# Chunk 0 of a delta-rule kernel: 64-token inverses from 16-token blocks by four 64-row products per head instead of seven of 32 rows

## The chip, the core and the metric

The program runs on one core of one Trainium2 chip. The metric is device time in microseconds of one execution. The engines are named as in the profile: PE is the matrix engine, PEld its weight loads, DVE the vector engine, ACT the scalar engine, POOL GpSimd, SP the engine that issues most transfers.

## What is computed

Four batches of eight heads of 768 tokens and head size 48 go through a delta rule, and its result through a feed-forward layer with 384 inputs and 2048 hidden units.

```python
k_n = k / (norm(k) + 1e-06)
for t in range(S):
    y[:, :, t] = einsum('bhd,bhde->bhe', q[:, :, t], state)
    v_old = einsum('bhde,bhd->bhe', state, k_n[:, :, t])
    state = state + beta_t * einsum('bhd,bhe->bhde', k_n[:, :, t], v_t - v_old)
x = y.transpose(0, 2, 1, 3).reshape(B * S, H * D)
h = x @ w_in
out = (h * sigmoid(h)) @ w_out
```

## The kernel before

**Chunks and halves.** The 768 tokens are worked in six chunks of 128, each chunk in two halves of 64 (`W`). Within a half the recurrence is written as a triangular system for each of the 32 pairs of batch and head (`BH`): the scores of the keys with each other above the diagonal, times a step size for each token, give a unit triangular matrix of 64x64, whose inverse (scaled by the step sizes) is kept in `xi`, 64 rows for each head, `[128, 2 groups, 16 heads, 64]`. With it, `inner` turns values into updates, `update` adds these to the state, and `keys`, `old`, `new` and `first_outputs` read state and scores. The two halves of a chunk and the two groups of batches lie crosswise on the upper and lower 64 partitions (`on`, `heads`).

**Inverses of chunk 0.** The score blocks go out to memory (`block_out`, by `issue`) and come back with one head's 32x32 block a partition (`block_in`, L570). `invert_first` (L651) scales them by the step sizes (L656), runs 15 rank-one steps on the two 16x16 corners of every block at once (L664, L668), scales again (L671), and transposes the result twice on DVE (L678 and L682) to have tokens on partitions again. Then three stages, made by generators, join 16 to 32 tokens on PE: `corner` (L705), `turned` (L721) and `straight` (L734), and `merge_half` (L794) twice joins 32 to 64. Every stage writes products of 32 rows into two PSUM banks, which ACT and DVE copy out (`by_act` L532, `by_dve` L535, and L712). For each half that is seven products a head and 32 heads; a product of 32-bit data is two records of the trace. `joins(0)` runs as a whole before the first half of chunk 0 is solved. `joins(1)`, for the second half, is drawn piecewise by the script.

**Step sizes.** `norm_steps(0)` (L391 to L421, DVE) makes the key norms, `spread` and the sizes by slot. `block_steps` (L430) brings `spread` to one head's block a partition by a product (`pg`, L433) and a copy on ACT (`step`, L438). `first_queries(b)` transposes queries of batch `b` on PE (L488), copies on ACT (L498), multiplies scores (L517) and masks them on DVE (L527, b below 2) or copies on ACT.

**Order of work.** Each engine does its instructions in program order: every instruction is pinned behind the last one on its engine (`pin`), and transfers on SP stand in one line (`in_line`), some of them behind the landing of the one before (`linked`). `busy` puts filler products on PE (L336); in the loop of the inverse's steps they wait for a DVE step. The weights `w_in` and `w_out` are fetched in eight pieces each and narrowed piece by piece (`fill`; ACT L224 and L225, DVE L229 and L233, POOL L237); a `hidden` product (L1029) of step r needs piece r // 2. POOL also squares keys (L373), clears `xi` (L1303), the identity blocks (L552) and `slab` (L1337), copies `pick` (L679) and scales values (`size_half`, L445).

**The script.** After `joins(0)` a text gives the order of everything else around chunks 0 and 1, word by word: `s` a step of `solve` (first `inner` L828 of the first half, then `first_outputs` L872 twice, `update` L848, `keys` L816, `old` L894, `new` L907), `jN` N steps of `joins(1)`, `r` a step of the feed-forward of chunk 0 (three `hidden` products), `f` a step of narrowing, `b` the begin of a piece, `q` the queries of chunk 1, `W` and `w` fetches, `h` the scaling of the second half's values. L1326 masks the query scores of batches 2 and 3, ahead of the script.

Of the kernel before, what the change touches and what calls it, by code (L numbers as in the profile page):

```python
# [19 lines left out]
def kernel(  # L20
# [19 lines left out]
    W = 64  # L40
# [223 lines left out]
    AT_G = 0  # L264
    AT_X = AT_G + (T + 1) * T
    AT_UP = AT_X + SLAB
    AT_LOW = AT_UP + BH * T
    AT_LAST = 2 * HFF * HM
    assert AT_LOW + BH * T // 2 <= 3 * HFF * HM and BH * T <= HFF * HM
# [56 lines left out]
    second = const.tile([P, 1], FP32, name="second")  # L326
    pin(nc.vector.tensor_reduce(out=second[:], in_=pick[:, T // 2 : T], axis=AX.X, op=ALU.add))
    xi = const.tile([P, 2, HH, W], FP32, name="xi")
    xis = [xi[:, g] for g in range(2)]
    crossed = const.tile([P, HH, T], FP32, name="crossed")  # L330

# [209 lines left out]

    def block_room(c):

        if c == 0:
            g, x = (sum_room[:, at : at + T * T] for at in (AT_G, AT_X))
        else:
            g = work.tile([P, T * T], FP32, name="g", tag="g", bufs=1)[:]
            x = (
                sum_room[:, AT_LAST : AT_LAST + T * T] if c == 1
                else work.tile([P, T * T], FP32, name="x", tag="x", bufs=1)[:]  # L550
            )
# [3 lines left out]
        blocks[c] = (tc.dram_tile([P, T, T], FP32, name=f"blocks{c}"), g, x)  # L555
# [89 lines left out]
    Q, ys = T // 2, {}  # L645
# [4 lines left out]

    def invert_first(step):  # L651

        x = blocks.pop(0)[2]
        g2, x2 = corners(AT_G), corners(AT_X)
# [4 lines left out]
        for m in range(Q - 1, 0, -1):  # L659
# [14 lines left out]
        rows = [slice(T * j, T * (j + 1)) for j in range(NB)]  # L674
        low = sum_room[:, AT_LOW : AT_LOW + BH * Q].rearrange("p (n s) -> p n s", s=Q)
        y = sum_room[:, AT_G : AT_G + BH * T].rearrange("p (n s) -> p n s", s=T)
        up = sum_room[:, AT_UP : AT_UP + BH * T].rearrange("p (n t) -> p n t", t=T)
# [7 lines left out]
        both = work.tile([P, BH, T], FP32, name="xe_y", tag="g", bufs=1)  # L685
        xes[0], ys[0] = both[:], both[:].rearrange("p (g h) t -> p g h t", g=2)

        def heads(g, hf):
            for i in range(HH // 2):
                for e in range(2):  # L690
                    yield i, HH * g + 2 * i + e, hf ^ e ^ g

        def of_half(t, g, hf, k):
            return t[:, HH * g + (hf ^ k ^ g) : HH * (g + 1) : 2]

        def out_of(pl, to, width):
            return pl[to, 0 : HH // 2 * width].rearrange("p (n s) -> p n s", s=width)

        def corner(g, hf):

            pls = [bank(room, "pl") for room in (A, CC)]
            for i, n, k in heads(g, hf):
                for j in (2 * k, 2 * k + 1):
                    cols = slice(T * (j % 2), T * (j % 2 + 1))
                    pin(nc.tensor.matmul(  # L705
                        pls[k][rows[j], Q * i : Q * (i + 1)], lhsT=aps[0, g][0][rows[j], n % HH // H, n % H, cols],
                        rhs=low[rows[j], n, :], start=True, stop=True,
                    ))
                    yield
            for k in range(2):  # L710
                of = slice(W * k, W * (k + 1))
                pin(nc.vector.scalar_tensor_tensor(  # L712
                    out=of_half(y[of], g, hf, k)[:, :, 0:Q], in0=out_of(pls[k], of, Q), scalar=second[of],
                    in1=pick[of, 0:Q].unsqueeze(1).to_broadcast([W, HH // 2, Q]), op0=ALU.mult, op1=ALU.add,
                ))

        def turned(g, hf):

            pls = [bank(room, "pl") for room in (A, CC)]
            for i, n, k in heads(g, hf):  # L720
                pin(nc.tensor.matmul(  # L721
                    pls[k][rows[2 * k], T * i : T * (i + 1)], lhsT=up[rows[2 * k], n, :],
                    rhs=y[rows[2 * k], n, :], start=True, stop=True,
                ))
                yield
            for k, by in enumerate((by_act, by_dve)):
                by(of_half(xes[0][rows[2 * k]], g, hf, k), out_of(pls[k], rows[2 * k], T))

        def straight(g, hf):

            pls = [bank(room, "pl") for room in (A, CC)]
            for i, n, k in heads(g, hf):
                for j in (2 * k + 1, 2 * k):
                    pin(nc.tensor.matmul(  # L734
                        pls[k][rows[j], T * i : T * (i + 1)], lhsT=y[rows[j], n, :],
                        rhs=up[rows[j], n, :], start=True, stop=True,
                    ))
                    yield
            for odd in (1, 0):
                for k, by in enumerate((by_act, by_dve)):  # L740
                    j = 2 * k + odd
                    by(
                        of_half(xi[rows[j]].rearrange("p g h t -> p (g h) t"), g, hf, k)[:, :, T * odd : T * odd + T],
                        out_of(pls[k], rows[j], T),
                    )

        yield corner, turned, straight
# [3 lines left out]
    slab = sum_room[:, AT_X : AT_X + SLAB]  # L751
# [28 lines left out]

    def merge_half(g, hf, second):

        y = ys[0][:, g]
        pms = [bank(room, "px" if second else "py") for room in (A, CC)]
        for i in range(HH // 2):
            for e in range(2):
                n, k = 2 * i + e, hf ^ e ^ g
                even, odd = slice(W * k, W * k + T), slice(W * k + T, W * (k + 1))
                if second:
                    to, left, right = even, y[odd, n, :], xis[g][odd, n, T:W]  # L790
                else:
                    left = aps[0, g][0][even, n // H, n % H, T:W]
                    to, right = odd, xes[0][even, g * HH + n, :]
                yield pin(nc.tensor.matmul(  # L794
                    pms[k][to, T * i : T * (i + 1)], lhsT=left, rhs=right, start=True, stop=True
                ))
        for k, by in enumerate((by_act, by_dve)):
            e, half = hf ^ k ^ g, slice(W * k, W * k + T) if second else slice(W * k + T, W * (k + 1))
            of = pms[k][half, 0 : HH // 2 * T].rearrange("p (h t) -> p h t", t=T)
            by(xis[g][half, e::2, T:W] if second else y[half, e::2, :], of)  # L800
# [486 lines left out]
    def first_queries(b):  # L1287

        def evacuate(j, e, to, of):
            (mask if b < HB else by_act)(to, of)  # L1290

        turn(0, b, 1, M)
        score(0, b, (1,), (A, CC), evacuate)
# [42 lines left out]
    corner, turned, straight = next(inv)  # L1336
    pin(nc.gpsimd.memset(slab, 0.0))  # L1337

    def joins(hf, between=()):

        for stage in (
            corner(0, hf), corner(1, hf), turned(0, hf), turned(1, hf), straight(0, hf), merge_half(0, hf, False),
            straight(1, hf), merge_half(1, hf, False), merge_half(0, hf, True), merge_half(1, hf, True),
        ):
            yield from stage
            for what in between[:1]:
                what()
            between = between[1:]
# [4 lines left out]
    def sized():  # L1353
        size_half(0, pins[seen_on])
        begin_next()
# [88 lines left out]
    def script(text):  # L1444

        nonlocal pieces
        for word in text.split():
# [12 lines left out]
            elif what == "j":  # L1460
                go(rest, n)
            elif what == "q":
# [96 lines left out]
```

## Time and profile before

| What | us |
|---|---|
| three runs | 652.4, 662.53, 659.86 |
| their median | 659.86 |
| the profiled execution | 652.37 |
| its span, first to last instruction | 650.4 |
| PE busy | 627.6 (96%) |
| DVE busy | 397.6 (61%) |
| ACT busy | 213.8 (33%) |
| POOL busy | 90.9 (14%) |
| first rank-one scaling of chunk 0 (L656) starts | 20.71 |
| first join product (L705) starts | 33.37 |
| `inner` of the first half (L828) starts | 44.24 |
| first `hidden` product (L1029) starts | 52.34 |
| xT of the second half lands | 101.17 |

Times are from the span's start. A row of a timeline has start, length, engine, line, operation, `out<-in`, shape and count, and in brackets the idle time before it with what ended it; "issue" means that nothing in the profile shows what was waited for. The granted clock is the share of full speed that PE was allowed. Counts of matmuls are of records, and a few of them are missing in the trace.

### The profile page before, as it was taken

How to read it: one execution, taken by the hardware profiler on the slowest of the kernel's cores; microseconds unless marked ns; L12 is line 12 of the kernel's file. 1: busy time of each engine (PE TensorE's matmuls, PEld its weight loads, DVE VectorE, ACT ScalarE, POOL GpSimd, SP SyncE). 2: the span in 40 equal slices, each digit the busy share in tenths (PEclk: the TensorE clock that was granted, in tenths of full speed). 3: DMA queues.
4: the chain of work that ended last, by engine and by line, in shares of the span. 5: the costliest groups of instructions: out<-in, count | busy, mean ns of one | idle time of the engine just before them, and what ended most of it. 6: DMA issues, size and time to landing. Idle time of an engine off the chain costs nothing.

```text
span 650.4 us, 21395 instructions
## 1 busy us (share of the span) xinstructions
PE 627.6 (96%) x9416; PEld 548.0 (84%) x9416; DVE 397.6 (61%) x911; ACT 213.8 (33%) x497; POOL 90.9 (14%) x92
## 2 busy tenths in 40 slices
PE   7878899999989999999999999999999999999997
PEld 5577778756779989989989989989989989889997
DVE  5875689997764987453986453987454974103112
ACT  2455663332342122451122452122451122451111
POOL 5023631334101020010020010020011000000000
PEclk9979999999989999999999999999999999999999
DMA  9876534250288324268324268324173024100101
GB/s 136 209 165 206 192 75 104 98 97 3 53 154 148 58 73 60 50 136 143 59 76 57 48 131 146 61 74 60 28 153 72 10 65 60 40 13 1 25 0 25
DMA packets 145676, 54.70 MB, mean 84 GB/s; under 512 B 117152, under 2 KB 138912, under 8 KB 145584
## 3 DMA queue, kind: packets, MB, share of 16 engines
q1 hardware_dynamic: 143136, 52.93, 39.6%
q8 instruction: 74, 1.21, 0.8%
q10 hardware_dynamic: 2448, 0.41, 0.4%
q14 instruction: 18, 0.15, 0.1%
HBM read 40.14 MB, written 11.01 MB: 79 GB/s over the span
## 4 chain that ended last, share of the span: by engine, by line
PE 91%; DMA 2%; issue 2%; DVE 2%; ACT 1%; SPq 1%; DVEq 0%
PE phid L1029 38%; PE px L1136 16%; PE py L1136 12%; PE po L1064 5%; PE pb_c L828 3%; PE pa L517 2%; PE pb_c L816 2%; PE pyc L907 2%; PE pb_c L1064 2%; PE pb_c L848 1%; PE pb_c L336 1%; PE pyc L894 1%; DMA kb<-in_k_dram 1%; PE pt L488 1%; PE py L770 1%
## 5 line engine op out<-in xcount | busy, mean ns | idle before, releaser
L1029 PE MATMUL phid<-xT,w_in 128*128 128x256 f32 x1152 | 260.1, 383 | 2.1 <-DMA xT<-part 2.0
L1029 PEld LDWEIGHTS phid<-xT,w_in 128*128 128x128 f32 x1152 | 216.9, 191 | 34.4 <-issue 3.0
L1039 ACT ACTIVATE gT<-phid 128x512 f32<-128x512 f32 x88 | 52.5, 597 | 149.8 <-PE phid L1029 145.2
L615 DVE SCALAR_TENSOR_TENSOR rank<-g,step,x 128x31 f32<-128x31 f32 (+15 forms) x124 | 49.8, 401 | 35.8 <-DMA g<-blocks 32.3
L1118 DVE TENSOR_TENSOR sums_of_g<-gT 128x384 f32<-128x384 f32 (+1 forms) x60 | 29.9, 518 | 59.0 <-ACT gT L1039 48.4
L1136 PE MATMUL py<-w_out,sums_of_g 128*128 128x192 f32 x320 | 56.8, 329 | 0.0
L1136 PE MATMUL px<-sums_of_w,sums_of_g 128*128 128x192 f32 x320 | 56.8, 329 | 0.0
L1136 PEld LDWEIGHTS px<-sums_of_w,sums_of_g 128*128 128x128 f32 x320 | 52.2, 190 | 0.5
L1136 PEld LDWEIGHTS py<-w_out,sums_of_g 128*128 128x128 f32 x320 | 52.2, 190 | 0.4
L620 DVE TENSOR_TENSOR x<-x,rank 128x31 f32<-128x31 f32 (+15 forms) x124 | 42.5, 343 | 4.3
L455 POOL TENSOR_TENSOR vf<-vf,n_slot 128x768 f32<-128x768 f32 x10 | 15.0, 1516 | 169.3 <-DMA vf<-in_v_dram 125.3
L476 DVE STREAM_TRANSPOSE kq<-stage 128x512 f32<-128x512 f32 x28 | 28.5, 1114 | 12.0 <-DMA stage<-in_q_dram 10.4
L532 ACT COPY xT<-pyc 48x128 f32<-48x128 f32 (+2 forms) x126 | 32.6, 259 | 1.6
L1136 PE MATMUL px<-sums_of_w,gT 128*128 128x192 f32 x160 | 28.4, 329 | 0.0
L1136 PE MATMUL py<-w_out,gT 128*128 128x192 f32 x160 | 28.4, 329 | 0.0
L1136 PE MATMUL px<-w_out,gT 128*128 128x192 f32 x160 | 28.0, 327 | 0.0
L1136 PEld LDWEIGHTS px<-w_out,gT 128*128 128x128 f32 x160 | 26.4, 190 | 0.5
L538 POOL COPY g<-x 64x256 f32<-64x256 f32 x4 | 5.0, 1241 | 154.5 <-DVE x L623 154.5
L1136 PEld LDWEIGHTS py<-w_out,gT 128*128 128x128 f32 x160 | 26.1, 190 | 0.3
L1136 PEld LDWEIGHTS px<-sums_of_w,gT 128*128 128x128 f32 x160 | 26.1, 190 | 0.2
L828 PEld LDWEIGHTS pb_c<-vf,xi 64*64 64x64 f32 x736 | 23.5, 138 | 3.2 <-issue 2.9
L1147 DVE TENSOR_TENSOR o<-o,kept 128x192 f32<-128x192 f32 (+1 forms) x29 | 11.5, 422 | 24.0 <-ACT kept L1144 24.0
(221 smaller groups left out, 921.6 us busy)
## 6 DMA issues: line engine op xcount, KB each, us to landing
vf<-in_v_dram SPq DMA_DIRECT2D x48, 96.0 KB, 3.2
out_dram<-o SPq DMA_DIRECT2D x42, 96.0 KB, 2.2
w_out<-in_moe_w_in_dram SPq DMA_DIRECT2D x4, 768.0 KB, 4.4
sums_of_w<-in_moe_w_out_dram SPq DMA_DIRECT2D x4, 768.0 KB, 5.9
blocks<-ap SPq DMA_DIRECT2D x44, 64.0 KB, 1.9
g<-blocks SPq DMA_DIRECT2D x5, 512.0 KB, 3.5
kb<-in_k_dram SPq DMA_DIRECT2D x12, 192.0 KB, 5.1
kb<-in_k_dram SPq DMA_DIRECT2D x24, 96.0 KB, 4.6
```

The source lines that it names most:

```text
L455: pin(nc.gpsimd.tensor_tensor(out=vf, in0=vf, in1=of, op=ALU.mult))
L476: pin(nc.vector.transpose(out=kqs[c, b][:, :, j, :].rearrange("p a (i m) -> p a m i", i=T), in_=src.rearrange("p a (m d) -> p a m d", d=D) ...
L517: pin(nc.tensor.matmul(pa[e][half, p * n * W : (p + 1) * n * W], lhsT=kq[rows, p, 0, half], rhs=kq[rows, p, js[0] : js[-1] + 1, half], sta ...
L532: return pin(nc.scalar.copy(to, of))
L615: pin(nc.vector.scalar_tensor_tensor(out=tv, in0=g[:, 0:m, m : m + 1].to_broadcast([P, m, n]), scalar=step[:, m : m + 1], in1=x[:, m : m + ...
L620: yield pin(nc.vector.tensor_tensor(out=x[:, 0:m, m:T], in0=x[:, 0:m, m:T], in1=tv, op=ALU.add))
L828: yield pin(nc.tensor.matmul(pz[rows, n * D : (n + 1) * D], lhsT=xis[g][rows, u * H + 2 * p + e, :], rhs=vfs[c][rows, hf, g * HB + u, p, : ...
L1029: pin(nc.tensor.matmul(ph[:, j * GT : (j + 1) * GT], lhsT=w_in[:, a, (2 * f + j) * P : (2 * f + j + 1) * P], rhs=xTs[c, hf][:, a, :], star ...
L1039: pin(nc.scalar.activation(out=hidden_of(c, hf, f), in_=ph[:], func=ACTF.Silu, scale=-0.5 if in_blocks(c) else 0.5))
L1064: pin(nc.tensor.matmul(pos[i][:, 0:DM], lhsT=hidden_of(0, hf, f // 2)[:, at : at + C], rhs=w_outs[f // HFF][:, f % HFF, :], start=(f == 0) ...
L1118: pin(nc.vector.tensor_tensor(out=sums_of_g[:, k, fs], in0=of[0], in1=of[1], op=op))
L1136: pin(nc.tensor.matmul(to, lhsT=at, rhs=quarter(f, *b) if isinstance(b, tuple) else sums_of_w[b][:, f], start=start and f == 0, stop=f == ...
```

## The change

The 32x32 blocks still come back as before, and the 15 rank-one steps stay. After them both transposes are of 512 elements; eight copies, spread over ACT, POOL and DVE, write the 16-token blocks and their transposes into 64x64 matrices with zeros elsewhere (`et` and `xi`, by a per-partition factor `of_rows`, 1 in one quarter of the rows). The 64-token inverse is then four products a head, each with 64 rows: `first` (scores times `et`, `mt`), `second` ((`mt` + 1) times `xi`), `third` and `fourth` (32 columns). The scores must therefore be zero at and below the blocks' diagonal, which four selects on POOL do in place (`above_blocks`). Memsets of `xi`, the `pick` copy and `merge_half` for chunk 0 go. Rooms in `sum_room` move; `eye`, `of_rows` and a helper lie in `crossed`, made by three small DVE operations at the start instead of one.

Besides: `block_steps(0)` is called between the transposes and the scores of the second `first_queries`; two turns of chunk 1's keys are made after each of steps 10 and 12 instead of one after each of steps 10, 12, 14 and 15; the masks L1326 move behind the first `s` of the script (word `a`); the fills between the joins move, and one `begin_next` is left out; the script's words up to `h` are ordered anew with the same numbers of `r` and `f`.

```diff
-    for t in xis:
-        pin(nc.gpsimd.memset(t, 0.0))
...
+    def above_blocks(g):
+        ap = aps[0, g][0][:].rearrange("p u h (q t) -> p (u h) q t", t=Q)
+        for rows in HALVES:
+            pin(nc.gpsimd.affine_select(
+                out=ap[rows], in_=ap[rows], pattern=[[0, HH], [Q, NQ], [0, Q]], compare_op=ALU.is_gt, fill=0.0,
+                base=0, channel_multiplier=-1,
+            ))
...
-        pin(nc.vector.transpose(out=low.rearrange("p n s -> p s n"), in_=x[:, 0:Q, :]))
-        pin(nc.gpsimd.tensor_copy(
-            out=y[:, :, Q:T], in_=pick[:, Q:T].unsqueeze(1).to_broadcast([P, BH, Q])
-        ))
-        pin(nc.vector.transpose(
-            out=up.rearrange("p n t -> p t n"), in_=x.rearrange("p s t -> p t s")
-        ))
+        def widen(to, of, q, by):
+            to, scale = to[:, :, Q * q : Q * (q + 1)], of_rows[:, q : q + 1]
+            if by == "act":
+                pin(nc.scalar.activation(out=to, in_=of, func=ACTF.Copy, scale=scale))
+            else:
+                engine = nc.vector if by == "dve" else nc.gpsimd
+                pin(engine.tensor_scalar(out=to, in0=of, scalar1=scale, scalar2=None, op0=ALU.mult))
+        pin(nc.vector.transpose(
+            out=turned[:, 0].rearrange("p n s -> p s n"), in_=x2.rearrange("p i s t -> p s i t")
+        ))
+        pin(nc.vector.transpose(
+            out=turned[:, 1].rearrange("p n t -> p t n"), in_=x2.rearrange("p i s t -> p t (i s)")
+        ))
+        for q, by in enumerate(("act", "pool", "act", "pool")):
+            widen(et, turned[:, 0], q, by)
+        for q, by in enumerate(("dve", "dve", "act", "pool")):
+            widen(xi[:].rearrange("p g h t -> p (g h) t"), turned[:, 1], q, by)
...
+        def first(g, hf):
+            pl = bank(A, "pl")
+            for i, n, rows in heads(g, hf):
+                yield pin(nc.tensor.matmul(
+                    pl[rows, W * i : W * (i + 1)], lhsT=aps[0, g][0][rows, n // H, n % H, :],
+                    rhs=et[rows, HH * g + n, :], start=True, stop=True,
+                ))
+            of = pl[:].rearrange("p (i s) -> p i s", s=W)
+            by_act(mt[:, g], of)
+            pin(nc.vector.tensor_tensor(
+                out=more[:, g], in0=of, in1=eye.unsqueeze(1).to_broadcast([P, HH // 2, W]), op=ALU.add
+            ))
+        def second(g, hf):
+            pl = bank(CC, "pl")
+            for i, n, rows in heads(g, hf):
+                yield pin(nc.tensor.matmul(
+                    pl[rows, W * i : W * (i + 1)], lhsT=more[rows, g, i, :], rhs=xis[g][rows, n, :],
+                    start=True, stop=True,
+                ))
+            for k, by in enumerate((by_act, by_dve)):
+                rows = HALVES[k]
+                by(of_half(g, hf, k, rows, slice(0, W)), pl[rows].rearrange("p (i s) -> p i s", s=W))
+        def third(g, hf):
...
+                    pl[rows, T * i : T * (i + 1)], lhsT=mt[rows, g, i, :], rhs=xis[g][rows, n, T:W],
...
+            by_act(z[:, g], pl[:, 0 : HH // 2 * T].rearrange("p (i t) -> p i t", t=T))
+        def fourth(g, hf):
...
+                    pl[rows.start : rows.start + T, T * i : T * (i + 1)], lhsT=mt[rows, g, i, 0:T],
+                    rhs=z[rows, g, i, :], start=True, stop=True,
...
+                pin(nc.vector.tensor_tensor(
+                    out=to, in0=to, in1=pl[rows, 0 : HH // 2 * T].rearrange("p (i t) -> p i t", t=T), op=ALU.add
+                ))
...
-    for b in range(2):
-        first_queries(b)
-        busy(1)
...
-    step = block_steps(0)
+    first_queries(0)
+    busy(1)
+    between = []
+    first_queries(1, lambda: between.append(block_steps(0)))
+    step, = between
+    busy(1)
+    for g in range(2):
+        above_blocks(g)
...
-        if n in (10, 12, 14, 15):
-            turn(1, (10, 12, 14, 15).index(n), 0, M)
+        if n in (10, 12):
+            for b in range(n - 10, n - 8):
+                turn(1, b, 0, M)
...
-    together(joins(0, [sized, none, none, filled(2), filled(1), none, none, filled(2), begin_next, none]))
-    masks(1, 0)
-    masks(1, 1)
+    pin(nc.gpsimd.memset(slab, 0.0))
+    together(joins(0, [sized, none, none, filled(3), none, begin_next]))
...
-        "s f3 s q s q b j20 j8 r j16 f j16 q f j20 r j4 f j32 j8 b j4 q j4 W7 r f r j16 j6 f j4 j8 f j8 f b j8 f j4 j8 r j12 e r f j99 h w2 ...
+        "s a s q s q f3 b j34 r f3 j34 r q f j34 r f2 q j34 W7 f r f b r f2 e r f h w2 ...
```

More of the change, by code (lines that the diff above doesn't have):

```diff
@@ L325 @@
         pin(nc.gpsimd.tensor_copy(out=pick[rows], in_=ident[rows, rows]))
-    second = const.tile([P, 1], FP32, name="second")
-    pin(nc.vector.tensor_reduce(out=second[:], in_=pick[:, T // 2 : T], axis=AX.X, op=ALU.add))
+    Q = T // 2
+    NQ = W // Q
     xi = const.tile([P, 2, HH, W], FP32, name="xi")
@@ L641, in invert @@
         read_up(c, up)
-    Q, ys = T // 2, {}
+    ys = {}
     def corners(at):
@@ L690, in heads @@
                 for e in range(2):
[L691 to L707, printed above, removed]
-                    ))
-                    yield
+                    yield i, 2 * i + e, HALVES[hf ^ e ^ g]
@@ L729, in straight @@
[L729 to L745, printed above, removed]
@@ L747, in invert_first @@
-        yield corner, turned, straight
-    slab = sum_room[:, AT_X : AT_X + SLAB]
+                rows = slice(W * k, W * k + T)
+                to = of_half(g, hf, k, rows, slice(T, W))
+                pin(nc.vector.tensor_tensor(
+                    out=to, in0=to, in1=pl[rows, 0 : HH // 2 * T].rearrange("p (i t) -> p i t", t=T), op=ALU.add
+                ))
+        yield first, second, third, fourth
+    slab = sum_room[:, AT_SLAB : AT_SLAB + SLAB]
     xTs, parts = {}, {}
@@ L779, in merge @@
                 (by_act, by_dve)[g](y[rows, g], of[rows])
[L781 to L800, printed above, removed]
     def of_heads():
@@ L1292, in first_queries @@
         turn(0, b, 1, M)
+        between()
         score(0, b, (1,), (A, CC), evacuate)
@@ L1333 @@
             busy(1, done, Sync)
-        if n in (10, 12, 14, 15):
-            turn(1, (10, 12, 14, 15).index(n), 0, M)
-    corner, turned, straight = next(inv)
-    pin(nc.gpsimd.memset(slab, 0.0))
+        if n in (10, 12):
+            for b in range(n - 10, n - 8):
+                turn(1, b, 0, M)
+    stages = next(inv)
     def joins(hf, between=()):
[L1341 to L1348, printed above, removed]
+        for stage in stages:
+            for g in range(2):
+                yield from stage(g, hf)
+                yield
+                for what in between[:1]:
+                    what()
+                between = between[1:]
     def filled(n):
@@ L1461, in script @@
                 go(rest, n)
+            elif what == "a":
+                masks(1, 0)
+                masks(1, 1)
             elif what == "q":
```

83 lines of the change are left out of this document (47 added, 36 removed).

## The prediction, made before the result was known

> **What bounds the kernel now.** I read the page first (sections 1 and 2), then the chain in order of time from 10 to 102 us, then a table of windows over the early stages, then the timelines of VectorE, GpSimd and SyncE around the first inversion.
>
> ```profile
> span 650.4 us, 21395 instructions
> PE   7878899999989999999999999999999999999997
> PEclk9979999999989999999999999999999999999999
> ```
>
> TensorE is full from about 100 us to the end; only the first five slices (16 us each) hold much idle PE, and slice 3 holds a low clock. Whatever the change does between 15 and 75 us moves the rest of the program by as much, since from 101 us PE is busy 99.7 of 102 us. So the price of the change is the shift of the first `hidden` products and of what follows them.
>
> ```profile
> 36.88 1.38 issue
> ...
> 40.52 1.86 issue
> ...
> 55.42 0.53 issue
> ...
> 59.26 1.25 issue
> ...
> 65.68 1.68 issue
> ```
>
> These lines of the chain are PE standing still although no row shows what it waits for. Between such gaps I count 124 (38.3 to 42.4), 131 (56.0 to 60.5) and 129 (60.5 to 67.4) matmul records, each with a weight load: some 256 instructions. The page lists 74 transfers of instructions with 1.21 MB on q8, 16 KB each. My reading: PE's program arrives in blocks of 256 instructions, and many tiny products use a block up faster (2.25 to 5.2 us) than the next one comes (4.1 to 6.9 us from start to start).
>
> ```profile
> 33.00:44.00 11.00, 7.62 (x448) 6.91 (x448) 8.21 (x17) 5.54 (x13) 4.67 (x3) 0.80 0.58 142
> 44.00:52.00 8.00, 8.00 (x229) 7.41 (x228) 5.46 (x10) 4.60 (x9) 1.92 (x1) 0.63 0.78 175
> 52.00:73.00 21.00, 17.45 (x469) 13.99 (x459) 12.28 (x22) 12.12 (x23) 5.91 (x4) 1.00 0.65 224
> ```
>
> Columns: window, its length, busy time (and count) of PE, weight loads, DVE, ACT, POOL, then the granted clock. The two halves of the inverses' joins lie in the first and third window. After the two long gaps the granted clock is 0.50 from about 39.5 to 49.9, so `inner` and `first_outputs` run at half speed.
>
> ```profile
> 132.11 1.87 POOL L237 TENSOR_TENSOR w_out<-w_out,sums_of_w 128x768 int32<-128x768 int32 x1 [1.61 <-ACT sums_of_w L225]
> 133.95 1.57 POOL L455 TENSOR_TENSOR vf<-vf,n_slot 128x768 f32<-128x768 f32 x1
> ...
> 132.32 1.86 DVE L620 TENSOR_TENSOR sums_of_w<-sums_of_w,rank 128x175 f32<-128x175 f32 x1
> 134.22 1.47 DVE L615 SCALAR_TENSOR_TENSOR rank<-g,step,sums_of_w 128x156 f32<-128x156 f32 x1
> ```
>
> A DVE operation on two SBUF tensors, normally 0.35 us, lasts until the POOL operation beside it has ended; one DVE operation slips in between two POOL operations. A one-input POOL operation does it too: L671 takes 0.98 us beside the L679 copy (29.98 to 30.61), where 1024 elements of the same kind (L623) take 1.22. DVE reading PSUM is not held (L881 0.54 at 50.1 beside L237 at 49.7).
>
> **The change, part by part** (profiled execution: 652.37 us, a span of 650.4 and 2.0 around it).
>
> *Step sizes earlier.* `step` was ready at 20.42 (L438), but L656 also waits for `g`: its DMA (L570) is issued at 17.21 and such transfers land in 3.4 to 4.6 us, so not before 20.6, and L656 starts at 20.71. Gain 0.0 to 0.1. The price is a wait: `pg` now stands on PE ahead of the second query's scores and of all filler behind them, and it needs `spread` (17.67 in the trace). SP's and POOL's queues are not passed.
>
> *The selects (`above_blocks`), four on POOL, 64x1024 each.* Rows: affine select 128x128 0.292, 64x64 0.235, so 0.9 ns an element and 1.1 us each; a 128x1024 memset takes 0.95 (lower bound), the POOL copy of 64x256 1.24 (upper bound, 5 us each). They wait only for the block transfers out of `ap` (issued 11.06 to about 14.5, landing in 3.1 to 4.1), so they run from about 15.3 to 20. There DVE does the norm steps, all on SBUF, which sit on the chain. By the rows above only some four of these get through until 20. What is left then is 0.8 us of `spread`, 0.7 of sizes and 1.35 of masks: L656 starts near 23.0 instead of 20.7. In a formula 18.7 + 4s, s being a select's time. `spread` is ready at 20.9, PE stands from 17.5 to 20.95, and its 15.3 us from the second scores (18.1) to the first join product (33.4) shift by 2.8, some of them perhaps at half clock. The removed memsets of `xi` (1.84) held nobody. **+3.2** with the widening below; bounds 0 (no lock) and +11 (s = 3) to +19 (s = 5).
>
> The Trainium skill, SBUF — State Buffer, section "SBUF: two separate sides", says that VectorE with two SBUF inputs and a GpSimd operation that reads SBUF exclude each other for a whole instruction. The trace agrees (1.86 us for L620); by that rule the selects cost the 2.3 us of DVE above, without it nothing.
>
> *Widening.* One 512-element transpose (1.06) in place of one of 1024 (1.93): -0.9. Before the first product four copies of 128x512 must exist, two on ACT (0.59 each) and two on POOL (0.63 by L679): the first product can start 2.5 us after L671's end, 33.7 without the selects, against 33.4 before, where PE's filler was the limit. DVE's two copies to `xi` may be held by POOL's; they are needed only by the second product, 2 us later.
>
> *Joins, first half.* 224 products of 32 rows become 128; each is two records, so 448 become 256. A 64-row record on four quadrants takes 14 to 18 ns (L848: 64 in 0.87; L816: 62 in 1.14), on two quadrants 31 at full clock (L828: 31 in 1.92 at half clock, 48 wide). The new ones use two quadrants; I take 35 ns for 64 columns, 22 for 32: 2.2, 2.2, 1.4, 1.4 us, 7.2 in all, about the old work. Chain from the first product F: `more` (DVE, 0.69 as L500) at F+1.8, second product to F+4.4, copies to F+5.1, third to F+5.85, fourth to F+7.1; DVE must do `filled(3)` (0.55 + 0.96) before the four additions (0.43 each as L535), so `inner` starts at F+7.7. Before it was 33.4 to 44.2, 10.9, with 3.24 of gaps. **-3.2** (bounds: -5.0 with 17 ns a record, 0 if the gaps stay).
>
> *The half clock.* From 44.3 to 49.9 it costs 2.8 us. The new joins leave PE idle for shorter times, but PE also waits for `spread`. I take half: **-1.5** (0 to -2.8).
>
> *Joins, second half.* Same products between the `hidden` steps. The three gaps, 3.46 us, need blocks used in under 4.1 to 6.9 us; about 340 records over 18 us make a block last 6.7. Work may grow by 0.5. Copies (0.7 to 1.4 us per stage) lie beside one `hidden` step (1.49). **-3.0** (-4 to 0). The masks moved behind `inner` (1.29 on DVE) lie beside `first_outputs(0)` and cost 0. If that cover goes, 1.29.
>
> Sum: +3.2 - 3.2 - 1.5 - 3.0 = -4.5, so 647.9 for an execution like the profiled one. The three runs of before are 652.4, 659.86 and 662.53; the profile is 7.5 below their median. I add half of that: 651.6.
>
> **Rivals.**
> 1. *The selects hold nobody.* For it: they might run in gaps of DVE; against it: L671 and L620. Front +0.3, the rest as above: -7.4, 645.0, with the half spread 648.7.
> 2. *The selects are long.* Their pattern has three levels with runs of 16, and the 64x256 copy is at 4.8 ns an element. Each 1 us more costs 4 us, since DVE's inversion and PE's filler queue behind. The front is then 4s - 1.2, the gain behind it 7.7, so it decides from s = 2.2. At s = 3 it is +3.1, 655.5, with the half spread 659.2. Against it: the affine rows, and L679, which writes runs of 16 at 1.2 ns an element.
> 3. *The gaps are not the supply of instructions.* Then they stay with as many waits: the first half gains 0, the clock 0, the second half 0, and the front costs 3.2: 655.6, or 659.3. Against it: 124, 129 and 131 records between them.
>
> The Trainium skill, Runtime: NRT & Kernel Launch, section "Instruction fetch mechanics", describes blocks of 256 instructions but holds the crossing to be mostly hidden; by that the third rival would be right. The five gaps with no releaser, 6.7 us, speak against it.
>
> **How the numbers follow.** Forecast 0.53, first rival 0.22, second 0.12, third 0.13. A measurement of this kernel tells about 2% (13 us) from no change, and all cases lie within it. The bounds taken together reach -11.8, 640.6 at the low end. At the high end the second and third rivals with half the spread reach 659, and s somewhat longer 661. Range 641 to 661. Below 646.7 (2% under the median) lie about a third of rival 1 and a tenth of the forecast: 0.13. Above 673 only rival 2 at s = 5 or so: 0.02.
>
> **What would show it.** L656 near 23 and norm steps stretched beside selects of 1.1 us (rival 1: L656 at 20.7; rival 2: selects over 2.2). The first 64-row product at 36 to 37.5, `inner` less than 8 us later, 64-wide records spaced 30 to 40 ns. Gaps without releaser between 52 and 73 below 1 us in sum, and a granted clock at 44 to 50 over 0.63. The forecast is wrong if the first `hidden` product does not come before 52.3, or if that lead is lost again before 101 us, for instance because weight pieces narrowed by POOL and DVE come late.

## The result, and the profile after

| | before | after |
|---|---|---|
| median of 20 runs each, same chips | 655.74 us (651.31 to 662.80) | 661.50 us (658.38 to 665.51) |
| profiled execution, span | 652.37, 650.4 us | 661.66, 659.9 us |
| mean granted TensorE clock | 0.990 | 0.984 |

The ratio is 1.0107 (95% interval 1.0083 to 1.0132): about 7 us slower, where 4.5 us of gain was forecast. It is within the 2% that count as no change, but it is a loss. Medians take in a few slow executions (over 1.5% above the fastest of the same kernel) and ratios leave them out, so the two can differ by some tenths of a per cent.

The first two parts of the page of after, cut to TensorE:

```profile
span 659.9 us, 20625 instructions
...
PE   8689999999999998999999999999999999999997
PEclk9689999999999998999999999999999999999999
```

Apart from the last, four slices are not full: the first three, and slice 16 (247 to 264 us). Before it was the first five and slice 12. The low clock sits one slice earlier, in slice 2 (16 to 33 us).

The first line of the page's chain of work that ended last, of before and then of after:

```profile
PE 91%; DMA 2%; issue 2%; DVE 2%; ACT 1%; SPq 1%; DVEq 0%
PE 54%; DVE 18%; DMA 9%; SPq 4%; issue 2%; ACT 2%; POOL 1%; POOLq 0%; DVEq 0%
```

In after 18% of the chain lies on VectorE, most of it in the column steps of the later chunks' inverses (L635, L640). The point on full TensorE, in the part on why the prediction was wrong, comes back to it.

The table of windows of after (window, length, busy time and count of PE, weight loads, DVE, ACT, POOL, granted clock, DMA share, GB/s):

```profile
20.00:33.00 13.00, 9.59 (x84) 6.21 (x85) 11.52 (x41) 2.15 (x9) 2.04 (x2) 0.56 1.19 229
33.00:44.00 11.00, 10.31 (x67) 6.51 (x65) 5.15 (x11) 5.57 (x10) 6.30 (x4) 0.74 0.62 132
44.00:52.00 8.00, 6.24 (x191) 5.86 (x191) 3.71 (x6) 4.07 (x8) 1.48 (x1) 1.00 0.93 175
52.00:73.00 21.00, 20.52 (x530) 18.12 (x526) 14.63 (x25) 14.42 (x24) 7.40 (x4) 1.00 0.56 184
```

The first of these windows in before:

```profile
20.00:33.00 13.00, 11.59 (x114) 7.79 (x113) 11.12 (x34) 6.88 (x17) 0.63 (x1) 1.00 0.98 222
```

Its granted clock was 1.00; now it is 0.56. 33 to 44 us held the first half's joins before (448 matmul records in the window); now it holds 67 records of transposes, scores and fillers, and the joins begin only at 44.9. In the last window TensorE is busy for 20.52 of 21 us, where it was busy for 17.45; but it holds other work now, since `hidden` begins only at 61.12.

The timeline of VectorE in before, at the norm steps and the first scaling:

```profile
15.54 0.19 DVE L401 SCALAR_TENSOR_TENSOR nr<-nt,nr 128x32 f32<-128x32 f32 x1
...
15.99 0.18 DVE L406 TENSOR_SCALAR n<-nt 128x32 f32<-128x32 f32 x1
...
16.67 0.19 DVE L408 TENSOR_TENSOR nt<-nr,beta_tok 128x32 f32<-128x32 f32 x1
16.90 0.77 DVE L411 SCALAR_TENSOR_TENSOR spread<-nr,nt 32x32 f32<-32x32 f32 x4
...
20.71 0.69 DVE L656 TENSOR_TENSOR sums_of_w<-sums_of_w,step 128x512 f32<-128x512 f32 x1 [0.95 <-ACT beta_tok L352]
```

The timelines of VectorE, GpSimd and TensorE of after (start, length, operation, in brackets the idle time before it and what ended it):

```profile
15.58 0.19 DVE L411 TENSOR_TENSOR nt<-nt,nr 128x32 f32<-128x32 f32 x1
15.81 1.43 DVE L412 SCALAR_TENSOR_TENSOR nr<-nt,nr 128x32 f32<-128x32 f32 x1
17.27 0.19 DVE L416 TENSOR_TENSOR nt<-nr,ss 128x32 f32<-128x32 f32 x1
17.49 1.41 DVE L417 TENSOR_SCALAR n<-nt 128x32 f32<-128x32 f32 x1
...
19.40 1.07 DVE L419 TENSOR_TENSOR nt<-nr,beta_tok 128x32 f32<-128x32 f32 x1
20.51 1.99 DVE L422 SCALAR_TENSOR_TENSOR spread<-nr,nt 32x32 f32<-32x32 f32 x4
...
25.04 0.68 DVE L685 TENSOR_TENSOR sums_of_w<-sums_of_w,step 128x512 f32<-128x512 f32 x1
...
15.69 6.41 POOL L675 TENSOR_SCALAR_AFFINE_SELECT ap<-ap 64x1024 f32<-64x1024 f32 x4 [4.62 <-ACT kq L509]
36.45 3.39 POOL L712 TENSOR_SCALAR sums_of_w<-turned,crossed 128x512 f32<-128x512 f32 x2 [14.35 <-DVE turned L714]
...
22.65 0.60 PE L444 MATMUL pg<-pick,spread 128*128 128x32 f32 x2 [4.94 <-DVE spread L422]
44.90 1.29 PE L740 MATMUL pl<-sums_of_w,ap 64*64 64x64 f32 x37 [0.75 <-ACT sums_of_w L709]
```

The four selects (`above_blocks`, L675) take 1.56 us each. Beside each of them one VectorE operation that needs 0.18 or 0.19 us in before lasts until the select has ended, so `spread` is ready at 22.5 instead of 17.7, and TensorE stands for 4.94 us behind the moved `pg`. L685, the old L656, starts at 25.04 instead of 20.71. The last row shows what ends the wait before the first join product: a copy on ScalarE, the widening L709. It stands behind ScalarE's copies of transposes, and these wait for TensorE.

Milestones of each profile, in us. "First scaling" is L656 of before and its counterpart; "lead" is how much earlier than in before the first silu of chunk 0's second half starts (103.2 us there):

| | first scaling | first join product | `inner` | first `hidden` | `update` | lead at 103 | span |
|---|---|---|---|---|---|---|---|
| before | 20.71 | 33.37 | 44.24 | 52.34 | 73.45 | 0 | 650.4 |
| after | 25.04 | 44.90 | 53.48 | 61.12 | 78.16 | -4.1 | 659.9 |
| e1_no_selects | 20.92 | 35.80 | 45.62 | 53.58 | 70.63 | +2.5 | 651.1 |
| e2_before_selects | 25.77 | 41.57 | 52.64 | 62.07 | 85.32 | -12.1 | 663.6 |
| e3_selects_on_act | 20.73 | 35.64 | 44.56 | 53.14 | 70.17 | +2.9 | 650.0 |
| e4_no_fillers | 24.75 | 41.75 | 51.12 | 59.95 | 76.98 | -2.4 | 656.3 |
| e6_widen_on_dve | 20.68 | 34.92 | 43.36 | 51.56 | 68.60 | +4.1 | 653.2 |

A profile is one execution, up to 4.2 us from its median here: places are read from profiles, ends from ratios.

### The profile page after: what moved, and what is told of

The parts are those of the page before. It is cut to its first block, busy times and chain, and to the rows that moved or that the text cites. A ratio compares the mean times of both kernels' runs of the same rounds, so it can differ in the third digit from the quotient of the medians.

```text
span 659.9 us, 20625 instructions
## 1 busy us (share of the span) xinstructions
PE 634.3 (96%) x9032; PEld 552.4 (84%) x9032; DVE 400.3 (61%) x903; ACT 214.8 (33%) x492; POOL 99.7 (15%) x96
## 4 chain that ended last, share of the span: by engine, by line
PE 54%; DVE 18%; DMA 9%; SPq 4%; issue 2%; ACT 2%; POOL 1%; POOLq 0%; DVEq 0%
PE phid L1048 18%; PE px L1155 9%; DVE rank L635 7%; PE py L1155 7%; DVE x L640 6%; PE po L1083 5%; DMA up<-x 2%; DVE sums_of_g L1137 2%; DMA g<-blocks 2%; PE pb_c L847 2%; DMA xe<-low 2%; SPq L102 2%; PE pb_c L835 2%; PE pa L528 2%; PE pyc L926 2%
## 5 line engine op out<-in xcount | busy, mean ns | idle before, releaser
L635 DVE SCALAR_TENSOR_TENSOR rank<-g,step,x 128x31 f32<-128x31 f32 (+15 forms) x124 | 49.8, 401 | 39.6 <-DMA g<-blocks 36.1
L640 DVE TENSOR_TENSOR x<-x,rank 128x31 f32<-128x31 f32 (+15 forms) x124 | 42.5, 343 | 4.3
L487 DVE STREAM_TRANSPOSE kq<-stage 128x512 f32<-128x512 f32 x28 | 28.4, 1107 | 11.7 <-DMA stage<-in_q_dram 11.7
L1155 PE MATMUL px<-w_out,gT 128*128 128x192 f32 x160 | 29.7, 341 | 0.0
L1155 PEld LDWEIGHTS px<-w_out,gT 128*128 128x128 f32 x160 | 28.1, 200 | 0.5
```

The source lines that it names most:

```text
L487: pin(nc.vector.transpose(out=kqs[c, b][:, :, j, :].rearrange("p a (i m) -> p a m i", i=T), in_=src.rearrange("p a (m d) -> p a m d", d=D) ...
L635: pin(nc.vector.scalar_tensor_tensor(out=tv, in0=g[:, 0:m, m : m + 1].to_broadcast([P, m, n]), scalar=step[:, m : m + 1], in1=x[:, m : m + ...
L640: yield pin(nc.vector.tensor_tensor(out=x[:, 0:m, m:T], in0=x[:, 0:m, m:T], in1=tv, op=ALU.add))
L1155: pin(nc.tensor.matmul(to, lhsT=at, rhs=quarter(f, *b) if isinstance(b, tuple) else sums_of_w[b][:, f], start=start and f == 0, stop=f == ...
```

## The experiments

Each ran in five rounds against the kernel before; its edits are against the kernel after unless said otherwise. The runs of before beside them had medians of 653.2 to 654.2 us.

**e1_no_selects** leaves out the clearing of the score blocks.

```
-    for g in range(2):
-        above_blocks(g)
```

> The changed kernel without the four selects on POOL (so the scores below the blocks stay in, and the inverses of chunk 0 are not the right ones). Theory 1, the selects hold DVE's norm steps and through them PE: L685 starts near 20.9 instead of 25.0, pg near 18 instead of 22.7, PE has no gap of 4.9 us there and no half clock between 20 and 36, the first 64-row product comes at 36 to 38 (POOL's two widening copies, 3.4 us, set it) instead of 44.9, and the whole is 8 to 12 us faster than the changed kernel, so about 0.985 to 0.995 of the kernel before. Rival A, the widening and the joins cost the time: first product not before 42, ratio to the kernel before over 1.005. Rival B, the time is lost after 105 us: first product early, but ratio still 1.00 to 1.01.

Measured: 653.43 us, ratio 0.9999 (0.9979 to 1.0019). The first scaling is back at 20.92. So the selects cost about 7 us, all of the loss. The 8 to 12 us that were expected did not come: what is left is no faster than before, though the lead at 103 us is 2.5 us. An early first product and a ratio of 1.00 is what rival B said of a loss after 105 us; e6 to e12 look for it there.

**e2_before_selects**: the kernel before, with the same four selects put in ahead of its `block_steps(0)`.

> The kernel before with the same four selects added at the same place of the program (they clear only scores that its joins do not use), everything else as it was. Theory 1: the norm steps are held by 4 x 1.55 us less what gets through, the first scaling moves from 20.7 to about 24.5 to 25, the first join product from 33.4 to 38 or later, and the whole is 4 to 9 us slower than before (1.006 to 1.014). Rival A: under 1.002.

Measured: 662.63 us, ratio 1.0148 (1.0118 to 1.0179): 9.7 us, with none of the new products, and just above the 4 to 9 us that were expected. The selects alone make the loss. They do so without the moved `pg` too: here TensorE stands for 4.67 us until 23.61, at a filler that waits for VectorE's masks (L527), and the granted clock is 0.62 from 20 to 33 us.

**e3_selects_on_act**: the clearing as eight ScalarE copies with a factor of 0 or 1 per row (`keep`, four tiny VectorE operations), placed ahead of the inverse.

```
-            pin(nc.gpsimd.affine_select(out=ap[rows], in_=ap[rows], ...
+        for q in range(NQ):
+            pin(nc.scalar.activation(out=ap[:, :, q], in_=ap[:, :, q], func=ACTF.Copy, scale=keep[:, q : q + 1]))
```

> The changed kernel with the selects made on ACT, as eight copies with a factor for each partition (0.37 us each, after the queries' scores of batch 3), POOL free. Theory 1: as without selects, with 3 us more on ACT ahead of the first narrowing: first scaling near 20.9, PE at full clock between 20 and 33, first product at 35.5 to 38, ratio to the kernel before 0.985 to 0.997. Rival A: over 1.005.

Measured: 655.11 us, ratio 1.0017 (0.9982 to 1.0051): like e1, with the whole work done, and again short of the gain that was expected (0.985 to 0.997). The windows of e3:

```profile
20.00:33.00 13.00, 10.32 (x107) 6.65 (x106) 11.07 (x35) 8.98 (x23) 0.91 (x1) 1.00 1.08 223
33.00:44.00 11.00, 9.06 (x242) 7.77 (x242) 5.48 (x8) 6.09 (x12) 7.17 (x6) 1.00 0.58 130
```

The granted clock is 1.00 in both, against 0.56 and 0.74 in after. In its timeline the products of the first half:

```profile
35.64 2.08 PE L743 MATMUL pl<-sums_of_w,ap 64*64 64x64 f32 x64 [0.70 <-POOL sums_of_w L715]
38.30 2.08 PE L757 MATMUL pb_c<-xi,mt_and 64*64 64x64 f32 x64 [0.58 <-DVE mt_and L749]
...
41.33 2.05 PE L769 MATMUL pl<-xi,mt 64*64 64x32 f32 x62 [0.43 <-DVE xi L552]
43.31 1.24 PE L779 MATMUL pb_c<-sums_of_w,mt 64*32 64x32 f32 x64
```

The first product now waits for GpSimd's widening (L715), and the third, of 32 columns, takes as long as one of 64.

**e4_no_fillers** takes the seven filler matmuls (`busy(1, done, Sync)`) out of the inverse's loop, to see whether TensorE's own queue, at half clock, holds the joins back.

> The changed kernel without the seven filler products inside the loop of inverse steps (no result uses them). If PE's queue of fillers at half clock sets the first product, it moves from 44.9 to 40 to 41 (POOL's second widening copy ends at 39.8), and the whole is 2 to 4 us faster than the changed kernel (ratio to before 1.002 to 1.008), unless the clock then stays at half through the joins, which would take back up to 4 us. If DVE and POOL alone set it, the first product stays at 44 to 45 and the ratio at 1.009 to 1.013.

Measured: 657.99 us, ratio 1.0069 (1.0043 to 1.0095). The first join product comes at 41.75, 3.15 us earlier, and the time falls by about 2.5 us; the clock stays at 0.58 and 0.66. Of the 11.5 us by which after is late there, some 3 are these fillers, most of which run at half clock. Without them TensorE stands for 2.00 us until ScalarE's widening has ended, so more than its own queue holds the joins back.

The pair e3 and e4 also tells about the gaps without a releaser. Two stretches of the chain, of e3 and then of e4 (start, length, what):

```profile
48.58 0.34 PE py L894 x3
48.92 0.77 issue
49.69 0.92 PE py L894 x43
```

```profile
55.21 0.58 PE py L891 x16
55.79 0.94 issue
56.73 0.69 PE py L891 x30
```

L894 and L891 are the same products, `first_outputs`. Counted from the start of the program, both gaps come after 725 matmul records. e4 has left 14 records out ahead of them, and the gap falls that much later in the loop. So it keeps its place in the stream of instructions and not its place in the work. The gaps of before say the same: they come after 600, 727, 1107, 1235 and 1363 records, and e10 has them at the same five counts.

**e5_step_back**: e3 with the step's move undone.

```
-    between = []
-    first_queries(1, lambda: between.append(block_steps(0)))
-    step, = between
+    first_queries(1)
     busy(1)
...
+    step = block_steps(0)
```

> The kernel with the clearing on ScalarE, with the step sizes' matmul put back behind the second query's scores. Theory (the move is worth nothing, since the inverse's first scaling starts at 20.7 us with the step early and late alike): first 64-row product within 0.5 us of 35.6, time within 0.3% of the kernel before. Rival (TensorE stands behind the step's matmul, so the move costs): first product 1 to 2 us earlier, ratio to the kernel before 0.997 or less. Second rival (the move was needed): first product 1 us or more later.

Measured: 654.32 us, ratio 1.0019 (0.9988 to 1.0050); first product at 35.50. The move is worth nothing by itself.

**e6_widen_on_dve**: e3, with the four widenings ahead of the first product on VectorE, the second transpose behind them, and none on GpSimd.

```
-        for q, by in enumerate(("act", "pool", "act", "pool")):
+        for q, by in enumerate(("dve", "dve", "dve", "dve")):
...
-        for q, by in enumerate(("dve", "dve", "act", "pool")):
+        for q, by in enumerate(("act", "dve", "act", "dve")):
```

> The kernel with the clearing on ScalarE, and the four widenings that the first product reads on VectorE (0.5 us each by its widenings of before), none on GpSimd (1.7 us each). All theories: first 64-row product at 34.1 us (+-0.5) in place of 35.6, first hidden product 1.0 to 1.5 us earlier. Theory of the late gates (from the third chunk on the next chunk's inverse, which runs on VectorE and through two transfers, ends last, so what the first chunk gains is lost at the gates): the first silu of the third chunk is at most 1 us earlier than with the clearing alone moved, and the time is within 1 us of it (ratio to the kernel before 0.998 to 1.004). Rival (a gain of the first chunk carries through to the end): 1.5 us earlier at every chunk, ratio 0.994 to 0.998.

Measured: 651.61 us, ratio 0.9949 (0.9910 to 0.9987). The first product comes at 34.92, only 0.7 us earlier, because TensorE's fillers now end last (34.99); `hidden` comes 1.6 us earlier. The time is better than the theory of the late gates allowed, and on the rival's side. But the profile shows the gates at work. The lead is 4.1 us at 103 us and 6.3 at 229, and 0.3 at the third chunk's first silu (281.7 against 282.1). Three views of e6 there: the waits of TensorE (us in total, times, longest), the chain, and the window:

```profile
PE py L813 <- DMA xe<-low: 2.7, 2, 1.9
```

```profile
232.97 1.24 DVE x L649
...
234.32 1.26 POOL g L555
...
236.09 4.09 DMA up<-x
...
240.60 3.23 DMA xe<-low
...
243.88 1.81 PE py L813 x124
245.69 5.38 PE px L1158 x16
```

```profile
235.00:260.00 25.00, 22.29 (x471) 20.13 (x472) 14.68 (x44) 4.92 (x9) 3.74 (x5) 0.86 0.45 70
```

and the chain of before at the same place:

```profile
232.98 14.24 PE phid L1029 x66
247.23 1.38 PE py L770 x84
248.61 2.80 PE px L1136 x16
```

In before TensorE's own work ends last at this merge; from 110 to 580 us the waits of before show none for `xe`. In e6 TensorE arrives early, stands 1.93 us for the rows of the next chunk's inverse (VectorE's 31 column steps, GpSimd's turning, two transfers), and the next 16 records take 5.38 us in place of 2.80: the clock has fallen to half. The wait and the clock eat the lead. How much is lost scatters: in e5's profile the same wait at the fourth chunk is 2.25 us, since the transfer took 5.91 us in place of 4.09, and behind it a lead of 1.3 us at 325 us is a lag of 5.4 at 384.

**e7_before_short_chains** and **e8_act_short_chains** were meant to test that by shortening the chain.

```
-        for m in range(T - 1, 0, -1):
+        for m in range(T - 1, 0 if c == 1 else 8, -1):
```

> The kernel before, where the inverses of chunks 2 to 5 leave out their last eight of 31 column steps (16 VectorE instructions, 4.7 us of each chain by the trace; the inverses are not whole). Theory of the late gates: in the kernel before TensorE's own work ends last at those gates with about 0.9 us to spare, so it gains little: 0 to 2 us, ratio 0.997 to 1.0. Rival (the chains bound the kernel before as well): 4 chains by up to 4.7 us, ratio 0.975 to 0.99. Rival (the gain of the first chunk was never there): nothing said here.

> The kernel with the clearing on ScalarE, with the same column steps left out of the inverses of chunks 2 to 5. Theory of the late gates: with the chains short, the 2.5 to 3 us that the first chunk gained (its 16th silu, 2.9 us early) reaches the end: 2.5 to 4 us less than the kernel before with the same steps left out, ratio to the kernel before 0.990 to 0.996. Rival (the gain is lost elsewhere, or was a scatter of two profiles): as far from the shortened kernel before as the whole ones are from each other, which is 0.2% slower, +-0.35%.

Measured: 661.83 us, ratio 1.0065 (1.0018 to 1.0112), and 659.28 us, ratio 1.0090 (1.0058 to 1.0123). Both lost, so neither theory met. The edit did more than it said: other engines' work is handed out between the column steps, and with eight steps fewer it moved as well. That this lost the time is not shown by itself; e11, where that work stays in place, has 1.0021. The pair is inconclusive; e11 and e12 repeat it with that pacing kept.

**e9_up_before_low** (on e6) and **e10_before_up_before_low** (on before): in the inverses of chunks 2 to 5, `up` is sent as soon as it is scaled, ahead of the turning of rows and of `low`.

```
-        turn_rows(by_pool, slice(0, T // 4))
-        turn_rows(by_dve, slice(T // 4, T))
         low, up = ...
-        issue(low[:], g[EVEN])
         issue(up[:], x)
+        turn_rows(by_pool, slice(0, T // 4))
+        turn_rows(by_dve, slice(T // 4, T))
+        issue(low[:], g[EVEN])
```

> The kernel with the clearing on ScalarE and the widening on VectorE, where each later chunk's inverse (chunks 2 to 5) is sent out as soon as it is scaled, ahead of the turning of its rows on GpSimd and of the smaller transfer. Theory of the late gates: TensorE stands 1 to 2 us at the first merge of the third chunk (1.93 us without this) until the rows that come through the two transfers have landed; they should land about 1.3 us earlier (GpSimd's 1.25 us is taken out of the chain), the stand falls below 1 us, the half clock behind it goes, and the time falls by 1 to 4 us against the kernel without this: ratio to the kernel before 0.988 to 0.994. Rival (the gates do not matter): ratio 0.995 as without it.

> The kernel before, with the same transfer sent ahead. Theory of the late gates: TensorE does not stand at these gates in the kernel before in its profiled run, so it gains little: ratio 0.997 to 1.001. Rival (the transfers bound both kernels): ratio 0.988 to 0.994.

Measured: e9 646.49 us, ratio 0.9906 (0.9873 to 0.9939), against e6's 0.9949; e10 652.65 us, ratio 0.9982 (0.9947 to 1.0016). The same edit is worth nothing that can be told on before and about 3 us where TensorE arrives early. The intervals of e6 and e9 overlap, so the size is rough; the place is plain in the trace. The chain of e9 at the merge, and its window:

```profile
229.99 10.58 PE phid L1051 x49
240.56 1.22 PE py L813 x82
241.78 2.80 PE px L1158 x16
```

```profile
235.00:260.00 25.00, 25.00 (x672) 22.90 (x671) 15.46 (x46) 7.09 (x15) 1.15 (x2) 1.00 0.36 42
```

No wait, full clock. The lead over before is 4.9 us at 103 us, 6.7 at 229, 6.8 at 275, 6.7 at 372 and 465, 7.1 at 563: it reaches the end. The step from 4.9 to 6.7 is a loss of before: its profile has a wait of 1.69 us at 186 us and half clock from 190 to 193 us, and the profile of e10, which does the same work there, has a wait of 1.41 us and full clock. e9 leaves no work out and beats both kernels, before by 0.94% and after, by the two ratios, by some 2%.

**e11_before_short_paced** (on before) and **e12_dve_short_paced** (on e6) leave out the last eight column steps but keep the steps' pacing.

```
+            if c > 1 and m < 9:
+                yield
+                continue
```

> The kernel before, where the inverses of chunks 2 to 5 leave out their last eight column steps, but the other engines' work that is handed out between the steps stays where it was (in the earlier pair, leaving steps out also moved that work). Theory of the late gates: these chains have just enough room in the kernel before, so little changes: ratio 0.995 to 1.0.

> The kernel with the clearing on ScalarE and the widening on VectorE, with the same steps left out in the same way. Theory of the late gates: no stand of over 0.9 us at the first merge of the third chunk, full clock there, and the 4 us that this kernel is ahead at the end of the first chunk (its second half's first silu: 99.2 against 103.2 us) reach the end: 3 to 5 us under the shortened kernel before, ratio to the kernel before 0.987 to 0.993. Rival (the gain is lost somewhere else than at these chains): no better than with whole chains, ratio 0.995 or more.

Measured: e11 654.38 us, ratio 1.0021 (0.9992 to 1.0050), a little above the 0.995 to 1.0 that were expected; e12 645.20 us, ratio 0.9901 (0.9868 to 0.9933). Shorter chains are worth nothing to before and about 0.5% to e6, where the intervals overlap again. Two different ways of shortening the chain, e9 and e12, end within 1.3 us of each other. The theory of the late gates holds in e9, e10 and e12; the sizes are rough. The pages agree: of the chain that ended last, 14 to 19% lies on VectorE in e1, e3, e5 and e6, and 1% in e9 and e12.

## Why the prediction was wrong, step by step

The step that failed is the front: +3.2 us in the sum, until the first join product. It came at 44.90 instead of 33.37, +11.5. So the first `hidden` product came at 61.12, and not before 52.3. On VectorE the mechanism was the one predicted, and its formula came close: 18.7 + 4s gives 24.9 at the measured s of 1.56, and L685 started at 25.04. In part that is luck, since 0.42 us of it is a wait of VectorE for the second query's scores, which the formula leaves out. From there to the first product it took 19.9 us instead of 12.7. What was mis-sized or left out:

- *The select.* 1.56 us, not 1.1: 1.8 us over four of them. The prediction took the rows of small selects (0.9 ns an element) over the copy of 64x256 at 4.8; the truth is 1.5.
- *TensorE's stand.* 4.94 us, not 3.45. It does not take the moved `pg`: in e2 TensorE stands for 4.67 us without it.
- *The clock.* The prediction saw that the work behind the stand "perhaps" runs at half clock and set nothing down for that. This is the largest term: the clock was 0.50 from 21.7 to 38.7 us, and from `pg` to the first product it took 22.25 us, where the prediction shifts 15.3 us of work by 2.8 without stretching them. 0.75 us of the 22.25 are the wait for ScalarE. With the selects off GpSimd (e3) the clock was 1.00 all through and the first product came at 35.64. That the stand brings the half clock is argued from their order, in after and in e2; no run has one without the other there.
- *The widening on GpSimd.* 1.70 us each, not the 0.63 of a plain copy. In after it cost nothing there: it ended at 39.84, 5 us before the first product. In e3 it ends last, with the first product 2.3 us later than in before; on VectorE (e6) it gave back 0.7 of these, since the fillers then end last.

*Selects and VectorE exclude each other*: shown, by the rows above and by e1 and e2. The Trainium skill, SBUF — State Buffer, section "SBUF: two separate sides", gives this lock; the trace agrees for the operations with two SBUF inputs (1.43 us for 0.19). Rival 1 falls. Rival 2 had the right direction, selects longer than 1.1 us, but needed s over 2.2 to turn the sign; the sign turned at 1.56 because of the clock and because of the last point below.

*Joins of the first half*, -3.2: 8.6 us from the first product to `inner` in after, 8.9 in e3, against 10.9, so -2.0 to -2.3. The third product was taken at 22 ns a record and took 33.

*Half clock at 44 to 50*, -1.5: the half clock had moved into the front (17.0 us of it, where before had 10.3 from 39.6 to 49.9). From 44 to 52 us the clock was 1.00, but from `inner` to the first `hidden` it took 7.6 us in after and 8.6 in e3, against 8.1: -0.5 to +0.5. In e3 a gap of 0.77 us and waits for copies took the place of the half clock.

*Joins of the second half*, -3.0: from the first `hidden` to `update` 17.0 us in after and in e3, where it was 21.1: -4.1. The gaps of TensorE without a releaser went from 3.46 us to none in 52 to 73 us of after. Rival 3, by which they stay, falls. The gap that keeps its count in e3 and e4 speaks against it too, and in before 127 or 128 records lie between the gaps that the prediction counts at 124, 131 and 129.

*Full TensorE means that a shift carries through*: this assumption of the first part failed as well, on both sides. The terms above add up to +4.7 us at `update`, and the delay was 4.1 at 103 us, but the span of after is 9.5 longer in the profiles and some 7 by the ratio. The delay was 2.7 us at the last silu ahead of the third chunk's first merge (250.0 against 247.3) and 6.5 at the next one behind it (288.5 against 282.1): there TensorE stood twice, 1.19 and 0.76 us, for `xe`, which landed at 252.1 us (247.3 in before), and the clock was 0.93 in 235 to 260 us. That is slice 16 of the page. A lead does not carry either: the next chunk's inverse ends almost together with TensorE at each merge from the third chunk on, so a lead becomes a wait there, and the wait can cost clock. The lead of 2.5 to 2.9 us of e1 and e3 at 103 us is worth -0.7 and +0.4 us of span. With the chain shortened (e9, e12) leads of 4.9 and 5.6 us give 7.1 and 7.2 us, of which some 1.7 are the loss of before at 190 us. The step's move is worth nothing (e5), as predicted; the wait that the prediction names as its price comes from the selects.

*The median.* Half of the profile's distance from the median of three runs, 3.7 us, was added to the forecast. By 20 runs the profile of before lies 3.4 us under the median of 655.74, so this term was right.

## What to carry to other kernels

Before work is put on GpSimd, look at what VectorE does in those microseconds: an operation that "only fills idle GpSimd" can hold a serial VectorE chain for its whole length, and the same clearing on ScalarE cost nothing that could be told. A busy TensorE does not say that a shift will carry through: follow it through every later point where another chain joins, and give the slack there a number; a lead can be lost there, and a delay can grow. Where the matrix engine is made to wait, set down a price for the clock behind the wait and not for the wait alone.

## What the runs showed of the hardware

- VectorE's L417 of after has one SBUF tensor as input (128x32) and was still held for 1.41 us beside a select; it needs 0.18 in before.
- Multiplying 128x512 by a factor per row takes 1.70 us on GpSimd and 0.72 us on ScalarE (after), and 0.48 us on VectorE (e6).
- 64-row products of 32 columns took 33 ns a record (62 in 2.05 us), those of 64 columns 32.5 (64 in 2.08 us), both in e3. The fourth product, whose stationary side has 32 columns, took 19 ns (64 in 1.24 us).
- Waits of TensorE of 1.1 us (e5, at 241.6), 1.2 (after, at 250.0), 1.9 (e6) and 2.25 us (e5, at 343.4) were followed by a granted clock of 0.93, 0.93, 0.86 and 0.86 in their 25 us; one of 1.4 us (e1, at 242.8) by 1.00. The Trainium skill, TensorE: Matmul & The Clock Gate, Part 1, gives about 3.4 us of idleness as what brings the half clock; these runs show it after less, though a merge of 32-row products follows each wait. A wait of 1.69 us ahead of the scores of the keys, with no merge behind it (before, at 186.4), was followed by 0.93 in 180 to 205 us, and one of 1.41 there (e10) by 1.00. What decides is open.
- The unexplained gaps stand at fixed counts of instructions. The Trainium skill, Runtime: NRT & Kernel Launch, section "Instruction fetch mechanics", holds the crossing of blocks of 256 instructions to be mostly hidden; 0.4 to 2.6 us were seen here (e6; e2 and e11) where TensorE used up many small products quickly. That it is the fetch of instructions was not tried by itself.
